# The last-but-one block is scaled as soon as its divisors are there, and VectorE's closing products all come before its closing sums

## The chip, the cores and the metric

The kernel runs on one core of a Trainium2 chip. The metric is the device time of one execution in microseconds, as a median over runs; the profile of one further execution shows where the time goes. Engines are named as in the profile: PE is TensorE (products), PEld its weight loads, DVE is VectorE, ACT is ScalarE, POOL is GpSimd, SP is SyncE, on whose queue nearly all transfers are issued.

## The reference

The input is one sequence of 2048 tokens with 640 features in bfloat16.

```python
xn = layernorm(x)
qkv = xn @ wqkv                              # 32 heads of width 20
o = softmax(q @ k^T * 20**-0.5) @ v
s = o @ wo
h = sigmoid(xn @ w_gate) * (xn @ w_up)       # 1728 wide
g = silu(h @ w_down)
out = x + s * g
```

## The kernel before, in words

**Tiling.** Attention is worked in 32 blocks. A block is one group of four heads (a group's heads stand on four bands of 32 partitions) and one chunk of 512 queries. Blocks 0 to 23 go group by group; the last eight blocks alternate between the last two groups, chunk by chunk, so that block 30 is group 6 and block 31 group 7, both of the last chunk. The loop over the blocks' score tiles (128 keys by 512 queries, L977) keeps three engines full: TensorE makes scores, ScalarE takes the exponent of most of them (L176, into `pu`), and VectorE takes the exponent of the rest by bit operations: one conversion to 16-bit integers (L1382, `iv`) and three passes over up to four tiles at a time (L1081, L1084, and the multiply L1087, into `pb`). TensorE then multiplies the exponents with the values (L1029); the row of sums comes out beside the results in the same PSUM bank.

**Scaling of a block.** When all products of a block are done, `norm_a` copies the bank to `on` and sends the row of sums through memory to a tile of 128 partitions (`ld`, `lt`). `norm_b` takes the reciprocals (L1053) and sends them back, spread over the bands, as `rl`, in four copies (L1058). `norm_c` multiplies `on` by `rl` into `on_bf` (L1066) and copies the result onwards. For blocks up to 29 GpSimd does the multiply; for block 30 VectorE does, and four copies (L1070) bring its 80 rows together in the tile `o6`. The profile calls both `o6` and the last block's `o7` by the name `o`.

**Order of the work.** It is neither the program's loops nor the hardware that decide in which order each engine meets its instructions: a planner in the kernel steps a model of TensorE, ScalarE and VectorE in steps of 0.01 us and writes out, at build time, what each engine is given next. The planner keeps a list `gos` of blocks that wait to be scaled, each with the time from which their `rl` is expected. On VectorE the scaling is one of several candidates, tried after the closing chain and after the copying of a finished bank, ahead of ready parts of other work (`active`: projections, the gated unit, out-projection) and of the exponent passes. It is taken if its time has come and, besides, two conversions are ready or will be within 0.3 us, or if 8 us (`GO_WAIT`; 1.5 us for some blocks) have gone by. The engines follow the written order strictly.

**Out-projection.** The first three chunks' output rows are done in parts of 128 by 320 (`mk_out`): five products (L847), then on VectorE a product with the gate (L854, `otmp`) and a sum with the input (L858, on VectorE for the last parts, on GpSimd for the earlier ones), then a copy out (L860). In the last chunk, groups 0 to 5 are multiplied early (`mk_part`, L884, L890, L892). What is left for the end of the run is:

- `e_on` (L1126): ScalarE copies the last block's bank.
- `e_tr` (L1130): four transposes on TensorE; `div_scale` (L818, L820): VectorE divides by the sums; `e_back` (L1139): four transposes back; `e_o` (L1143): ScalarE copies the result to `o7`, in the buffer of `rl`.
- `early` (L1117): eight products with block 30's `o6`: four of 128 columns into the bank `rest`, four of 512 into the banks `mains`. `late_mm` (L1121): the same eight with `o7`, added up in the same banks. `tail_banks` takes the banks that the out-projection used before.
- VectorE multiplies `rest` and `mains` with the gate (L1163 twice, L1170 four times, `hT`), and VectorE or GpSimd adds the input and the earlier groups' part (L1166 on GpSimd twice; L1173 for each of the four row tiles). Four copies (L1177), two issued by SP and two by ScalarE, write the last 512 rows.

The two places that the change touches:

```python
if eng == "DVE" and gos and gos[0][0] <= now and (
        sum(x[3] <= now + 0.3 for x in dq) >= 2 or now > gos[0][0] + (1.5 if pressing(gos[0][1]) else GO_WAIT)):
```

```python
add = nc.vector if t4 > 1 else nc.gpsimd
add.tensor_tensor(out=tail[t4][:, 0:512], in0=tmps[t4], in1=xps[t4][:, 0:512], op=ALU.add)
```

Of the kernel before, what the change touches and what calls it, by code (L numbers as in the profile page):

```python
# [145 lines left out]
def kernel(  # L146
# [11 lines left out]
    nc = tc.nc  # L158
# [346 lines left out]
    T_GO, GO_AT, GO_WAIT = 0.08, 9.0, 8.0  # L505
    gos, pool_at, pool_from = [], [0.0], [0.0]
# [7 lines left out]
    NBLK = NG * NQC  # L514
# [7 lines left out]
    def pressing(b):  # L522
        return b >= PAIR and b % 2 == 1
# [443 lines left out]
    def claim_dve(had, not_j):  # L967
        for b in range(base(), min(NBLK, base() + 2)):
            if q_at.get(b, 1e9) > now:
                return None  # L970
            if n_left[b] >= (rule["dl"] if b < NBLK - 1 else rule["dle"]):
                js = [j for j in range(GH) if left[b][j] and j not in not_j]
                return take(b, max(js, key=lambda j: (j not in had, len(left[b][j]), j)), -1) if js else None
        return None
# [86 lines left out]
    def norm_c(b, on, rl, sync):  # L1061
        g, c = gc(b)
        if sync:
            nc.vector.memset(rl[0:1, 0:1], 1.0)  # L1064
        on_bf = w2.tile([P, QC], BF16, tag="on_bf", bufs=2, name="on_bf")
        (nc.gpsimd if sync else nc.vector).tensor_tensor(out=on_bf, in0=on, in1=rl, op=ALU.mult)  # L1066
        if b == NBLK - 2:
            last["o6"] = wk.tile([P, QC], BF16, tag="aq", bufs=4, name="o6")[0:GC, :]
            for j in range(GH):
                nc.sync.dma_start(out=last["o6"][j * DH:(j + 1) * DH, :], in_=on_bf[32 * j + 1:32 * j + 1 + DH, :])  # L1070
            return
        for j in range(GH):
            f = g * GC + j * DH
            nc.sync.dma_start(out=oD[f:f + DH, c * QC:(c + 1) * QC], in_=on_bf[32 * j + 1:32 * j + 1 + DH, :])
# [36 lines left out]
    def tail_banks():  # L1111
        if not tb:
            tb.extend([f for f in range(NFX) if f != pv_bank[0]])
            mains[2], mains[3], rest[0] = [bank[f] for f in tb]
# [5 lines left out]
    def late_mm(dst, t4, sl):  # L1120
        nc.tensor.matmul(dst, lhsT=last["o"][:, t4 * P:(t4 + 1) * P], rhs=wo_t[1][0:GC, sl], start=False, stop=True,  # L1121
                         skip_group_check=True)
# [28 lines left out]
    def tail_steps():  # L1151
        tail_banks()
        for _, _, f in fill:
            f()
        for t4 in range(4):
            late_mm(rest[0][:, t4 * EX:(t4 + 1) * EX], t4, slice(512, D))
        for t4 in range(4):
            late_mm(mains[t4], t4, slice(0, 512))
        tmps = [hfl[:, t4 * 2 * D:t4 * 2 * D + 1024].bitcast(FP32) for t4 in range(4)]
        tmp = hfl[:, 8 * D:8 * D + 8 * EX].bitcast(FP32).rearrange("p (t e) -> p t e", e=EX)  # L1160
        rests = rest[0].rearrange("p (t e) -> p t e", e=EX)
        for i in range(2):
            nc.vector.scalar_tensor_tensor(out=tmp[:, 2 * i:2 * i + 2, :], in0=rests[:, 2 * i:2 * i + 2, :], scalar=0.25,  # L1163
                                           in1=gq_last[i].rearrange("p (t u) -> p t u", u=D)[:, :, 512:D],
                                           op0=ALU.mult, op1=ALU.mult)
            nc.gpsimd.tensor_tensor(out=xr_last[i][:, :, 512:D], in0=tmp[:, 2 * i:2 * i + 2, :],  # L1166
                                    in1=wdf.rearrange("p (t u) -> p t u", u=D)[:, 2 * i:2 * i + 2, 512:D], op=ALU.add)
        for t4 in range(4):
            gqr = gq_last[t4 // 2][:, t4 % 2 * D:t4 % 2 * D + 512]
            nc.vector.scalar_tensor_tensor(out=tmps[t4], in0=mains[t4], scalar=0.25, in1=gqr,  # L1170
                                           op0=ALU.mult, op1=ALU.mult)
            add = nc.vector if t4 > 1 else nc.gpsimd
            add.tensor_tensor(out=tail[t4][:, 0:512], in0=tmps[t4], in1=xps[t4][:, 0:512], op=ALU.add)  # L1173
        for i, t4 in enumerate((0, 2, 1, 3)):
            r = slice(4 * (NQC - 1) * P + t4 * P, 4 * (NQC - 1) * P + (t4 + 1) * P)
            eng = nc.sync if i % 2 == 0 else nc.scalar
            eng.dma_start(out=out2[r, :], in_=tail[t4])  # L1177

    with tc.manual_schedule(engines={ENG.PE, ENG.Activation, ENG.DVE}):
# [6 lines left out]
        now = 0.0  # L1186
# [3 lines left out]
        dq = []  # L1190
# [53 lines left out]
        while chain or timed or gos or items or glu_items or any(it.i < len(it.ops) for it in active):  # L1244
# [62 lines left out]
            for eng in ("ACT", "DVE"):  # L1307
# [13 lines left out]
                    norm_pending = None  # L1321
                    continue
                if eng == "DVE" and gos and gos[0][0] <= now and (
                        sum(x[3] <= now + 0.3 for x in dq) >= 2 or now > gos[0][0] + (1.5 if pressing(gos[0][1]) else GO_WAIT)):
                    _, b, on, rl = gos.pop(0)
                    norm_c(b, on, rl, b < NBLK - 2)
                    if b == NBLK - 2:
                        free["DVE"] = max(now, pool_at[0] if pool_from[0] <= now else now) + 0.60
                        ev_at[("o6",)] = free["DVE"] + 2.5
                        continue  # L1330
                    free["DVE"] = now + T_GO
                    pool_from[0] = max(pool_at[0], now + T_GO + 0.15)
                    pool_at[0] = pool_from[0] + 1.3
                    o_at[b] = pool_at[0] + 4.0
                    continue
# [8 lines left out]
                if eng == "ACT":  # L1344
                    s = slots[nexp % 2]
                    if nexp < nfill and s["a"] is not None and s["at"] <= now:
                        jobs = s["a"]
                        m = len(jobs)
                        if pu_run(m) is not None:
                            u = pu_take(m)  # L1350
                            end, x = now, u
# [71 lines left out]
            if free["PE"] <= now:  # L1423
# [57 lines left out]
                if nxt == "F":  # L1481
# [3 lines left out]
                    while len(d_new) < rule["dmax"] and (dcur is not None or buf_free(iv_left, NIV)) \  # L1485
# [4 lines left out]
                        x = claim_dve([t[2] for t in dcur["jobs"]] if dcur else [], [y[2][2] for y in d_new])  # L1490
# [78 lines left out]
        assert not items and not glu_items and not any(it.i < len(it.ops) for it in active)  # L1569
        assert not timed and not gos  # L1570
        tail_steps()

# [28 lines left out]
```

## Time and profile before

| | |
|---|---|
| device time, median of 3 runs | 797.38 us (796.93 to 799.03) |
| span of the profiled execution | 798.3 us |
| PE busy | 760.7 us, 95% |
| DVE busy | 771.0 us, 97% |
| ACT busy | 769.2 us, 96% |
| POOL busy | 83.0 us, 10% |
| mean granted TensorE clock | 0.99 |

Busy times are those of the whole span; they hardly tell the stages apart, since three engines are full in all but the last few microseconds. A stretch is read better from the timeline of each engine, from the list of waits (who waited, on what, how long) and from the chain that ended last: it starts at the last instruction and goes back to whatever released each step. In the profile, an instruction's start and its length are those of the engine's work; one instruction's end overlaps a little with the next one's start on VectorE, so the pace is read from start to start.

### The profile page before, as it was taken

How to read it: one execution, taken by the hardware profiler on the slowest of the kernel's cores; microseconds unless marked ns; L12 is line 12 of the kernel's file. 1: busy time of each engine (PE TensorE's matmuls, PEld its weight loads, DVE VectorE, ACT ScalarE, POOL GpSimd, SP SyncE). 2: the span in 40 equal slices, each digit the busy share in tenths (PEclk: the TensorE clock that was granted, in tenths of full speed). 3: DMA queues.
4: the chain of work that ended last, by engine and by line, in shares of the span. 5: the costliest groups of instructions: out<-in, count | busy, mean ns of one | idle time of the engine just before them, and what ended most of it. 6: DMA issues, size and time to landing. Idle time of an engine off the chain costs nothing.

```text
span 798.3 us, 17147 instructions
## 1 busy us (share of the span) xinstructions
PE 760.7 (95%) x6509; PEld 274.5 (34%) x6509; DVE 771.0 (97%) x1276; ACT 769.2 (96%) x830; POOL 83.0 (10%) x99
## 2 busy tenths in 40 slices
PE   7899999999999999999999999999999999999994
PEld 5523223333333223333332333333333223333332
DVE  8899999999999999999999999999999999999995
ACT  7799999999999999999999999999999999999990
POOL 6100000000100000000000010000000002213132
PEclk9999999999999999999999999999999999999996
DMA  6521212124122122331113223342122332414301
GB/s 168 153 70 48 69 53 54 52 61 107 54 74 67 52 69 76 85 85 56 45 56 85 82 57 90 95 132 85 40 78 70 83 92 75 141 52 139 101 23 63
DMA packets 95875, 62.61 MB, mean 78 GB/s; under 512 B 36388, under 2 KB 89684, under 8 KB 95792
## 3 DMA queue, kind: packets, MB, share of 16 engines
q1 hardware_dynamic: 95504, 61.18, 27.3%
q8 instruction: 51, 0.84, 0.4%
q14 instruction: 32, 0.26, 0.1%
q10 hardware_dynamic: 288, 0.33, 0.1%
HBM read 47.84 MB, written 13.55 MB: 77 GB/s over the span
## 4 chain that ended last, share of the span: by engine, by line
ACT 49%; PE 33%; DVE 9%; issue 5%; DMA 3%; SPq 1%; POOL 0%; ACTq 0%; DVEq 0%; POOLq 0%
ACT pu L176 44%; PE pst L977 11%; PE pst L750 7%; PE pst L1029 6%; PE pst L788 4%; ACT tnh L176 3%; DVE iv L1382 3%; DVE pb L1087 2%; PE pst L847 1%; PE pst L610 1%; ACT td L176 1%; DMA lt<-ld 1%; DVE pb L1081 1%; PE pst L718 1%; PE pst L884 1%
## 5 line engine op out<-in xcount | busy, mean ns | idle before, releaser
L176 ACT ACTIVATE pu<-pst 128x1024 bf16<-128x1024 f32 (+2 forms) x690 | 735.6, 1322 | 3.6 <-PE pst L977 3.4
L1382 DVE TENSOR_SCALAR iv<-pst 128x512 int16<-128x512 f32 x492 | 324.7, 681 | 6.3 <-PE pst L977 3.9
L977 PE MATMUL pst<-q,kT 32*128 32x512 bf16 x2048 | 272.1, 383 | 14.2 <-ACT pu L176 9.1
L1029 PE MATMUL pst<-pu,v 128*21 128x512 bf16 x1556 | 177.7, 382 | 0.3 <-ACT pu L176 0.2
L977 PEld LDWEIGHTS <-kT 32*128 32x128 bf16 x2048 | 82.0, 91 | 255.2 <-issue 244.0
L1029 PE MATMUL pst<-pb,v 128*21 128x512 bf16 x984 | 152.5, 382 | 0.2 <-DVE pb L1087 0.2
L1087 DVE TENSOR_TENSOR pb<-iv,pb 128x2048 bf16<-128x2048 bf16 x123 | 151.1, 1228 | 0.5
L750 PE MATMUL pst<-xnT,wgu 128*128 128x512 bf16 x520 | 143.7, 382 | 1.3 <-DVE iv L1382 0.4
L1066 POOL TENSOR_TENSOR on_bf<-on,rl 128x512 bf16<-128x512 f32 x30 | 38.4, 1281 | 635.3 <-DVE rl L1064 549.5
L1081 DVE TENSOR_SCALAR pb<-iv 128x2048 int16<-128x2048 int16 x123 | 84.6, 688 | 0.2 <-PE pst L1029 0.2
L788 PE MATMUL pst<-wd,hT 128*128 128x320 bf16 x448 | 84.1, 302 | 0.4 <-DVE iv L1382 0.3
L1084 DVE TENSOR_SCALAR pb<-iv 128x2048 int16<-128x2048 int16 x123 | 84.0, 683 | 0.0
L1029 PEld LDWEIGHTS <-v 128*21 128x21 bf16 x2540 | 49.4, 91 | 85.1 <-issue 62.7
L750 PEld LDWEIGHTS <-wgu 128*128 128x128 bf16 x520 | 38.5, 97 | 62.7 <-issue 40.5
L788 PEld LDWEIGHTS <-hT 128*128 128x128 bf16 x448 | 35.6, 97 | 40.7 <-issue 30.2
L610 PE MATMUL pst<-xnT,wu 128*128 128x512 bf16 x160 | 46.3, 383 | 0.1
L176 ACT ACTIVATE tnh<-pst 128x512 bf16<-128x512 f32 (+1 forms) x56 | 45.2, 808 | 0.0
L758 DVE SCALAR_TENSOR_TENSOR hT<-tnh,pst 128x512 bf16<-128x512 bf16 x52 | 35.3, 678 | 0.2
L718 PE MATMUL pst<-wv,xnT 128*128 128x160 bf16 x280 | 27.7, 239 | 1.4 <-DVE v L285 0.8
L718 PEld LDWEIGHTS <-xnT 128*128 128x128 bf16 x280 | 20.2, 100 | 11.2 <-issue 9.9
L847 PE MATMUL pst<-xnT,v 128*128 128x320 bf16 x120 | 21.0, 300 | 0.7 <-DVE otmp L890 0.5
L1043 DVE COPY on<-pst 128x512 f32<-128x512 f32 x31 | 21.1, 682 | 0.3 <-PE pst L1029 0.2
(115 smaller groups left out, 354.8 us busy)
## 6 DMA issues: line engine op xcount, KB each, us to landing
rl<-rd SPq DMA_DIRECT2D x124, 64.0 KB
wgu<-in_B_w_gate_dram SPq DMA_DIRECT2D x24, 320.0 KB
wgu<-in_B_w_up_dram SPq DMA_DIRECT2D x24, 320.0 KB
gq_dram<-gqs SPq DMA_DIRECT2D x24, 160.0 KB
xnT<-gq_dram SPq DMA_DIRECT2D x10, 320.0 KB
xt<-in_A_x_dram SPq DMA_DIRECT2D x16, 160.0 KB
oD<-on_bf SPq DMA_DIRECT2D x120, 20.0 KB
wd<-in_B_w_down_dram SPq DMA_DIRECT2D x1, 2080.0 KB
```

The lines of the kernel that those rows point to most:

```text
L176: return nc.scalar.add_instruction(mybir.InstActivation(func=func, name=nc.get_next_instruction_name(), engine=ENG.Activation, ins=[nc.sca ...
L610: nc.tensor.matmul(st["ps"], lhsT=wus[u][:, kd, i, :], rhs=xnT[:, c, kd, :], start=(kd == 0), stop=(kd == KD - 1))
L718: nc.tensor.matmul(st["ps"][:, i * 2 * GC:(i + 1) * 2 * GC], lhsT=xn_tok(tts[i], kd), rhs=wvs[pr][:, kd, :], start=(kd == 0), stop=(kd == ...
L750: nc.tensor.matmul(st[key][0:fs, :], lhsT=w[:, i, kd, ko * P:ko * P + fs], rhs=xnT[:, c, kd, :], start=(kd == 0), stop=(kd == KD - 1))
L788: nc.tensor.matmul(st["ps"][:, 0:HD], lhsT=hT[0:fsz[kf], kf, t4 * P:(t4 + 1) * P], rhs=wd[0:fsz[kf], kf, h * HD:(h + 1) * HD], start=(kf = ...
L977: nc.tensor.matmul(dst, lhsT=kTs[gc(b)[0] % 2][32 * j:32 * j + 32, kt * P:(kt + 1) * P], rhs=qts[b % 3][32 * j:32 * j + 32, :], start=True ...
L1029: nc.tensor.matmul(bank[pv_bank[0]][32 * j:32 * j + DH + 1, :], lhsT=lhsT, rhs=u["src"], start=first, stop=last, tile_position=(0, 32 * j) ...
L1066: (nc.gpsimd if sync else nc.vector).tensor_tensor(out=on_bf, in0=on, in1=rl, op=ALU.mult)
L1081: nc.vector.tensor_scalar(out=pb[:, 0, :, :].bitcast(I16), in0=iv, scalar1=0x7F80, scalar2=1, op0=ALU.bitwise_and, op1=ALU.bitwise_or)
L1084: nc.vector.tensor_scalar(out=pb[:, 1, :, :].bitcast(I16), in0=iv, scalar1=0x007F, scalar2=0x3F00, op0=ALU.bitwise_and, op1=ALU.bitwise_or)
L1087: nc.vector.tensor_tensor(out=pb[:, 1, :, :], in0=iv.bitcast(BF16), in1=pb[:, 1, :, :], op=ALU.mult)
L1382: nc.vector.tensor_scalar(out=d["iv"][:, j:j + w, :], in0=pst[:, F_POS[bk]:F_POS[bk] + w, :], scalar1=B_OFF, scalar2=0.0, op0=ALU.add, op1 ...
```

## The change

```diff
             gqr = gq_last[t4 // 2][:, t4 % 2 * D:t4 % 2 * D + 512]
             nc.vector.scalar_tensor_tensor(out=tmps[t4], in0=mains[t4], scalar=0.25, in1=gqr,
                                            op0=ALU.mult, op1=ALU.mult)
-            add = nc.vector if t4 > 1 else nc.gpsimd
+        for t4 in range(4):
+            add = nc.vector if t4 else nc.gpsimd
             add.tensor_tensor(out=tail[t4][:, 0:512], in0=tmps[t4], in1=xps[t4][:, 0:512], op=ALU.add)
-        for i, t4 in enumerate((0, 2, 1, 3)):
+        for i, t4 in enumerate((0, 1, 2, 3)):
...
                 if eng == "DVE" and gos and gos[0][0] <= now and (
-                        sum(x[3] <= now + 0.3 for x in dq) >= 2 or now > gos[0][0] + (1.5 if pressing(gos[0][1]) else GO_WAIT)):
+                        sum(x[3] <= now + 0.3 for x in dq) >= 2 or now > gos[0][0] + (1.5 if pressing(gos[0][1]) else GO_WAIT) or gos[0][1] == NBLK - 2):
```

It has two parts. In the planner, block 30 (`NBLK - 2`) is scaled as soon as its time in `gos` has come, whatever else VectorE has ready. In the last steps, VectorE makes its four large closing products (L1170) one after the other and only then adds; it takes three of the four large sums instead of two, so that GpSimd has one; and the output copies are issued in the order of the row tiles. The part at the end puts in one line, so lines behind it stand one further down in the changed kernel: L1173 becomes L1174, L1177 becomes L1178, L1382 becomes L1383.

## The prediction

> **What bounds the kernel now.** The page says that PE, DVE and ACT are each busy for 95 to 97% of the span, so no stage but an unbalanced one can be shortened by an edit this small. I therefore read three views of the end of the run, in this order: the chain of work that ended last, the waits, and the timelines of VectorE and of the DMA queue. The chain from 781.97 us on (start, length, what):
>
> ```profile
> 781.97 0.68 DVE on_bf L1066
> ...
> 785.09 1.91 DMA o<-on_bf
> ...
> 787.13 2.29 PE pst L1117 x8
> 789.42 0.44 PE pst L1121 x4
> 789.89 0.45 DVE hT L1163 x2
> ...
> 790.56 1.89 DVE hT L1170 x3
> 792.47 1.17 DVE xr L1173
> 793.64 0.61 DVE hT L1170
> 794.27 1.04 DVE xr L1173
> ```
>
> The end is one string: block 30 is scaled (L1066), its four copies to `o` are issued and land, the eight products L1117 and the eight L1121 follow, then VectorE's closing products and sums. It starts at the scaling. The waits of 770 to 799 us (who waited for whom: sum, times, longest) say what that costs:
>
> ```profile
> DVE hT L1163 <- PE pst L1121: 5.4, 1, 5.4
> PE pst L1117 <- DMA o<-on_bf: 4.7, 1, 4.7
> ACT o L1143 <- DVE on_bf L1066: 3.7, 1, 3.7
> ```
>
> VectorE stands still for 5.4 us and TensorE for 4.7 us, both because the scaling came late; ScalarE waits too, since its copy `o` reuses the buffer `rl` that the scaling reads. Was the scaling late because its data was late? The DMA queue and the stretches of half a microsecond (last two numbers: DMA share and GB/s; the third from the end is TensorE's clock) answer that:
>
> ```profile
> 769.84 1.71 SPq L1058 DMA_DIRECT2D rl<-rd  x4
> 782.68 3.12 SPq L1070 DMA_DIRECT2D o<-on_bf  x4
> ```
>
> ```profile
> 772.50:773.00 0.50, 0.50 (x10) 0.15 (x6) 0.50 (x1) 0.50 (x2) 0.00 (x0) 1.00 0.24 74
> 773.00:773.50 0.50, 0.50 (x6) 0.29 (x4) 0.47 (x2) 0.50 (x2) 0.00 (x0) 1.00 0.00 0
> ...
> 785.00:786.00 1.00, 0.00 (x0) 0.00 (x0) 0.00 (x0) 0.00 (x0) 0.00 (x0) 1.00 0.12 32
> 786.00:786.50 0.50, 0.00 (x0) 0.00 (x0) 0.00 (x0) 0.00 (x0) 0.00 (x0) 0.50 0.07 16
> ```
>
> The `rl` copies are issued from 769.84 us and nothing moves after 773.0, so the data was there nine microseconds before it was used. The second pair shows the clock halving near 786.0, after TensorE's last product ended at 782.41. And VectorE is full between (timeline):
>
> ```profile
> 773.04 1.23 DVE L1087 TENSOR_TENSOR pb<-iv,pb 128x2048 bf16<-128x2048 bf16 x1
> 774.18 0.48 DVE L854 SCALAR_TENSOR_TENSOR otmp<-pst,xnT 128x320 f32<-128x320 f32 x1
> 781.97 0.68 DVE L1066 TENSOR_TENSOR on_bf<-on,rl 128x512 bf16<-128x512 f32 x1
> 784.01 0.49 DVE L858 TENSOR_TENSOR wd<-otmp,wd 128x320 bf16<-128x320 f32 x1
> ```
>
> Its last work before the hole ends at 784.42 us (784.01 plus the usual 0.41 to the next start).
>
> **What the Trainium skill says.** "TensorE: Matmul & The Clock Gate", section "What's actually happening", says that about 3.4 us of idleness halve TensorE's clock; here it fell 3.6 us after the last product, which agrees. "SBUF — State Buffer", section "Who interferes with whom", says that a VectorE instruction with two SBUF inputs contends with a GpSimd instruction that reads SBUF, one with a single SBUF input does not. The trace agrees: L1066 (128x512, two SBUF inputs, GpSimd idle) takes 0.684 us, the same shape at L1173 takes 1.17 and 1.04 beside GpSimd's sums, while L1170, which reads PSUM and SBUF, stays at 0.679. "DMA: Bandwidth & Descriptors", section "Rules for kernel authors", advises to issue early and wait late; the 1.91 us of the last `o` copy, exposed now, are such a latency.
>
> **The change part by part.** I compared the two programs' instruction orders. Up to the VectorE multiply at 773.04 us they are alike on every engine, so only what follows can differ.
>
> *Scaling moved.* L1066 goes from behind the fifth of the last seven out-projection pairs (L854, L858) to ahead of the first. It starts at 774.18, where 773.04 ends; `rl` is there 1.2 us earlier, so the wait costs nothing. It takes 0.60 us there (781.97 to 782.57) and gives the same 0.60 back later. The copies' issues follow at 774.9 instead of 782.68; they took 3.12 us, the last starting 2.41 after the first, so the last starts at 777.3 and lands at 779.2. Behind them in the DMA queue stand only copies of finished output rows, for which no engine waits.
>
> *What the planner shifts with it.* The last multiply L1087 goes behind one more pair. VectorE from 774.18: scaling 0.60, pair 0.93 (774.18 to 775.11), L1081 and L1084 0.60 each, pair 0.97: L1087 runs from 777.88 to 779.1 instead of 776.43 to 777.66. The last four attention products wait for it and end near 779.6; before, they ended at 778.3. So `on` (0.59) is ready at 780.3 and the transposes L1130 (0.6) at 780.95, a full 1.2 us later. It costs nothing: VectorE has three pairs for that time, 779.02 to 781.86, and all products they need are issued. The 128x1536 exp becomes two (by the means of the rows 0.81 + 1.21 for 1.67, so 0 to 0.35 us); ScalarE ended at 777.8 and has until 779.1, so I take nothing.
>
> *New order at the end.* From 781.86: reciprocal and scaling of the last block (L818, L820) 0.69, to 782.55; two pairs, 1.86, to 784.4: VectorE's work is the same sum as before. L1139 transposes 782.65 to 783.1, `o` of the last block is copied 783.2 to 783.8. L1117 finds its data long there; its order of waits shows that its second 512-wide product needs the PSUM bank that the last L854 reads, which starts near 783.5 and releases at 784.0. From 784.05 three 512-wide products at 0.22 and four 128-wide at 0.07 give 785.0 (full-clock paces: five 128x512 products of L750 take 1.19 us in the chain and four 0.97; the four of L1139 take 0.42, one 0.23; at half clock the timeline has 0.42 and about 0.11), and with 0.2 us of latency L1163 starts at 785.2. Before: 789.89. That is 4.7 us earlier; 0.8 us of VectorE's hole stay. TensorE's longest rest is now about half a microsecond, so I take the full clock; half clock would add 3 × 0.2 + 4 × 0.04, about 0.8, and is the upper bound.
>
> *Closing products ahead of closing sums.* Before, 5.42 us pass from 789.89 to the end of the last sum at 795.31. After: two L1163 0.67, four L1170 at 0.62, 2.5, then three sums instead of two. GpSimd has one sum instead of two: it starts its small ones 0.57 after L1163, needs 1.36 for them and 1.3 for the large one, so ends 3.2 us after L1163 started, just when VectorE's first sum starts. The sums then take what L1066 takes: 0.60 + 0.60 + 0.68 = 1.9. Together 5.1, a gain of 0.3; if they still collide as now (1.1 each), 6.4, a loss of 1.0. I take 5.1, since GpSimd is done. The four output copies follow at 0.6 us; the last had 3.0 us from its sum's end to the end of the span, and I keep that.
>
> Sum: 4.7 + 0.3 = 5.0 us. 797.38 − 5.0 = 792.4.
>
> **The rivals.** (A) *TensorE still at half clock, or sums that still collide with GpSimd*: 0.8 or 1.0 us back, 793.2 to 793.4, both 794.2. For it: there are only some 20 short products between 782.4 and 785. Against: clock 1.00 for the 3.6 us of full idleness before. (B) *The output copies become the bound*: four of 160 KB issued in 1.9 us instead of 2.2; they moved at up to 300 GB/s, 0.55 us each, but 164 to 191 while draining, 0.86 each. A backlog of 0.3 to 1.0 gives 792.7 to 793.4. (C) *VectorE has no hole left*: L1163 at 784.5, 791.7. (D) *A new wait takes the old one's place*: the scaling, now early in a strict order, waits for `rl`; the multiplies for attention and all pairs stand behind it, TensorE waits for those, and the end moves one for one. To give no change (797.4) `rl` must land 1.2 + 5.0 = 6.2 us later than in the trace, to end slower by 0.3% (799.8) 8.6 us later. Against it stands the DMA silence from 773.0.
>
> **How the numbers follow.** Forecast 0.60 (791.9 to 793.0), A 0.14, B 0.10, C 0.10, D 0.06. The range 791.1 to 794.4 takes in C less 0.6 and both halves of A with 0.2 to spare (the runs of before lie 2.1 us apart, their median less uncertain); it leaves out D, A and B together, and some of C's low side, less than 2 in 10. The 0.3% lines are 795.0 and 799.8: faster takes all but D, 0.94; D is split into 0.04 the same and 0.02 slower.
>
> **What would show it.** Right: no wait of TensorE for `o<-on_bf`; L1066 near 774.2 with no idle before it; the `o` copies issued by 778; clock 1.00 at L1121; L1163 at 785.2 with VectorE idle about 0.8 before it; three VectorE sums at 0.7; span about 793.3. Wrong: idle VectorE before L1066, a last L1087 later than 779, a half clock at L1117, sums still near 1.1 us, or over 3.0 us from the last sum to the end.

## The result, and the profile after

| | before | after |
|---|---|---|
| device time, median of 4 runs | 797.42 us (796.93 to 799.03) | 792.61 us (791.69 to 793.10) |
| ratio, with its 95% interval | | 0.9935 (0.9918 to 0.9952) |
| span of the profiled execution | 798.3 us | 791.4 us |
| from the start of the instruction behind the last common L1087 (774.18 before, 772.59 after) to the end of the span | 24.1 us | 18.8 us |

The kernel is 4.8 us faster. The two spans differ by 6.9 us, but 1.6 us of that lie ahead of the first instruction that the change moves: the common L1087 started at 773.04 before and at 771.45 after, and at 773.13 in a second profile of the changed kernel. That is mostly scatter from one execution to the next: the profiled execution of the kernel before took 800.0 us, 2.6 above its median, and that of the changed kernel 793.1, 0.5 above. All comparisons below count from the scaling (L1066) or from the first closing product (L1163).

The chain that ended last, from the scaling on (start, length, what):

```profile
772.06 0.53 issue
772.59 0.69 DVE on_bf L1066
...
781.38 0.49 DVE wd L858
781.87 0.41 DVE otmp L854
782.28 0.04 issue
782.32 0.81 PE pst L1117 x3
783.13 0.24 PE pst L1121 x4
...
784.14 2.39 DVE hT L1170 x4
786.53 0.61 DVE xr L1174
```

The copies to `o` and the eight products L1117 after them are gone from it. Between the scaling and 782.28 stands VectorE's own work, and only three products L1117 are left: the one that waits for the last L854, and the two behind it. The waits from 770 us on (who, on whom: sum, times, longest):

```profile
ACT o L1143 <- PE pst L1139: 2.9, 1, 2.9
DVE hT L1163 <- PE pst L1121: 0.6, 1, 0.6
PE pst L1117 <- DVE otmp L854: 0.3, 1, 0.3
```

VectorE's 5.4 us ahead of L1163 are 0.6; TensorE's 4.7 us for `o<-on_bf` have left the list; ScalarE waits for TensorE's transposes, no longer for the scaling. The DMA queue, a stretch (third number from the end: TensorE's clock) and the timelines of VectorE and, in the last line, GpSimd:

```profile
768.54 1.71 SPq L1058 DMA_DIRECT2D rl<-rd  x4
773.30 3.10 SPq L1070 DMA_DIRECT2D o<-on_bf  x4
```

```profile
783.00:784.00 1.00, 1.00 (x9) 0.48 (x7) 0.61 (x2) 0.00 (x0) 0.04 (x1) 1.00 0.33 120
```

```profile
772.59 0.69 DVE L1066 TENSOR_TENSOR on_bf<-on,rl 128x512 bf16<-128x512 f32 x1
776.25 1.22 DVE L1087 TENSOR_TENSOR pb<-iv,pb 128x2048 bf16<-128x2048 bf16 x1
783.39 0.75 DVE L1163 SCALAR_TENSOR_TENSOR hT<-pst,gql 128x256 f32<-128x256 f32 x2 [0.60 <-PE pst L1121]
784.06 2.47 DVE L1170 SCALAR_TENSOR_TENSOR hT<-pst,gql 128x512 f32<-128x512 f32 x4
786.46 1.89 DVE L1174 TENSOR_TENSOR xr<-hT,wd 128x512 bf16<-128x512 f32 x3
```

```profile
785.32 1.27 POOL L1174 TENSOR_TENSOR xr<-hT,wd 128x512 bf16<-128x512 f32 x1
```

The `o` copies are issued by 776.4, and the first L1117 starts at 781.40; TensorE is at full clock when it makes L1121; three sums take 1.89 us together, where two took 1.17 and 1.04 before. GpSimd's one large sum ends at 786.59 us, 0.13 after VectorE's first begins.

### The profile page after: what moved, and what is told of

Same layout as the page of the kernel before. It is cut to its first block, busy times and chain, and to the rows that moved or that the text cites. A ratio compares the mean times of both kernels' runs of the same rounds, so it can differ in the third digit from the quotient of the medians.

```text
span 791.4 us, 17148 instructions
## 1 busy us (share of the span) xinstructions
PE 756.8 (96%) x6509; PEld 272.6 (34%) x6509; DVE 770.5 (97%) x1277; ACT 768.5 (97%) x831; POOL 81.4 (10%) x98
## 4 chain that ended last, share of the span: by engine, by line
ACT 50%; PE 33%; DVE 9%; issue 5%; DMA 1%; SPq 1%; POOL 0%; DVEq 0%; ACTq 0%; POOLq 0%
ACT pu L176 45%; PE pst L977 11%; PE pst L750 7%; PE pst L1029 5%; PE pst L788 4%; ACT tnh L176 3%; DVE iv L1383 2%; DVE pb L1087 2%; PE pst L610 2%; PE pst L847 1%; ACT td L176 1%; DVE pb L1081 1%; DVE pb L1084 1%; PE pst L884 1%; DVE xn L384 0%
## 5 line engine op out<-in xcount | busy, mean ns | idle before, releaser
L1383 DVE TENSOR_SCALAR iv<-pst 128x512 int16<-128x512 f32 x492 | 324.8, 681 | 5.2 <-PE pst L977 2.9
L1087 DVE TENSOR_TENSOR pb<-iv,pb 128x2048 bf16<-128x2048 bf16 x123 | 151.3, 1230 | 0.5
L1066 POOL TENSOR_TENSOR on_bf<-on,rl 128x512 bf16<-128x512 f32 x30 | 38.4, 1280 | 633.4 <-DVE rl L1064 564.0
L1084 DVE TENSOR_SCALAR pb<-iv 128x2048 int16<-128x2048 int16 x123 | 83.9, 682 | 0.0
L847 PE MATMUL pst<-xnT,v 128*128 128x320 bf16 x120 | 21.1, 301 | 0.7 <-DVE otmp L890 0.5
```

The lines of the kernel that those rows point to most:

```text
L1084: nc.vector.tensor_scalar(out=pb[:, 1, :, :].bitcast(I16), in0=iv, scalar1=0x007F, scalar2=0x3F00, op0=ALU.bitwise_and, op1=ALU.bitwise_or)
L1087: nc.vector.tensor_tensor(out=pb[:, 1, :, :], in0=iv.bitcast(BF16), in1=pb[:, 1, :, :], op=ALU.mult)
L1383: nc.vector.tensor_scalar(out=d["iv"][:, j:j + w, :], in0=pst[:, F_POS[bk]:F_POS[bk] + w, :], scalar1=B_OFF, scalar2=0.0, op0=ALU.add, op1 ...
```

## The experiments

The kernels ran in three jobs, each on one chip and timed beside the kernel before, whose median was 798.76, 798.29 and 797.82 us in them. Where two variants are compared by time, they are of the same job unless the text says otherwise. A diff is against the changed kernel unless it says otherwise.

### The changed kernel once more

> The changed kernel itself, as the measure for the other three runs. Both theories: 792.4 us and within 1 us of it; from the start of the scaling of block 30 to the start of the first closing product (L1163) 10.8 us, from there to the end of the last closing sum 5.0 us.

792.99 us (791.27 to 795.91) against 798.76 before, ratio 0.9927 (0.9902 to 0.9952). Scaling at 774.27, L1163 at 785.06, end of the last sum at 790.02: 10.8 and 5.0 us. This is the measure for the other kernels of the first job: the scaling alone, the closing order alone, and, further below, the kernel that takes away the wait that is left.

### The scaling alone

```diff
-        for t4 in range(4):
-            add = nc.vector if t4 else nc.gpsimd
+            add = nc.vector if t4 > 1 else nc.gpsimd
...
-        for i, t4 in enumerate((0, 1, 2, 3)):
+        for i, t4 in enumerate((0, 2, 1, 3)):
```

> The planner's part alone; the closing products and sums stay in the order of before, two sums on GpSimd. Theory (the late scaling held up the end): 792.5 to 793.1 us, that is 4.4 to 4.9 below the kernel before; 10.8 us from the scaling to L1163, then 5.4 us to the end of the last sum, VectorE's two large sums at 1.0 to 1.2 us each. Rival (the closing order brings most of the gain, the scaling only moves a wait): 796 to 797 us, with a wait of some 4 us on TensorE or VectorE at another place.

793.61 us (792.77 to 796.53), ratio 0.9935 (0.9912 to 0.9957): 5.2 us below the kernel before, where the whole change brings 5.8 in the same job. Both this gain and the time lie somewhat above what was expected. Its timeline at the end:

```profile
782.64 0.76 DVE L1163 SCALAR_TENSOR_TENSOR hT<-pst,gql 128x256 f32<-128x256 f32 x2 [0.60 <-PE pst L1121]
785.22 1.16 DVE L1173 TENSOR_TENSOR xr<-hT,wd 128x512 bf16<-128x512 f32 x1
787.02 1.04 DVE L1173 TENSOR_TENSOR xr<-hT,wd 128x512 bf16<-128x512 f32 x1
```

The scaling is at 771.85, so L1163 follows after 10.8 us, and the last sum ends 5.4 us after that. The scaling alone brings nearly all, so the rival is wrong.

### The closing order alone

```diff
-... or gos[0][1] == NBLK - 2):
+...):
```

> The order of the closing products and sums alone; block 30 is scaled where it was before. Theory: 796.9 to 797.2 us, 0.2 to 0.5 below the kernel before, not to be told from it; TensorE still waits 4.7 us for the copies to o and VectorE 5.4 us; L1163 to the end of the last sum 5.0 us instead of 5.4, sums at 0.6 to 0.7 us. Rival (the closing order brings most of the gain): 793 to 794 us.

798.24 us (797.28 to 800.34), ratio 0.9994 (0.9980 to 1.0007): no difference that can be measured, though the median is 0.5 us lower. Its two large waits are those of the kernel before, number for number:

```profile
DVE hT L1163 <- PE pst L1121: 5.4, 1, 5.4
PE pst L1117 <- DMA o<-on_bf: 4.7, 1, 4.7
```

L1163 starts at 789.74 and the last sum ends at 794.69: 5.0 us, as forecast. In this one profile the span ends 3.5 us after that, where all other profiles of the study have 2.96 to 3.05. Its cause is open; the closer output copies don't explain it, since the changed kernel issues them as closely and has 3.05.

### Who makes the closing sums

Three kernels change only the last lines of the changed one: two sums on GpSimd, none, and each sum right behind its product. The first diff shows two of them, one added line each.

```diff
-            add = nc.vector if t4 else nc.gpsimd
+            add = nc.vector if t4 > 1 else nc.gpsimd    # two_gpsimd_sums
+            add = nc.vector                             # no_gpsimd_sum
```

```diff
-        for t4 in range(4):
             add = nc.vector if t4 else nc.gpsimd        # sums_between: in the loop of the products
```

> The changed kernel with two of the four large closing sums on GpSimd, as before, but all products still ahead of the sums. Theory (the two engines hold each other up when both sum from SBUF): VectorE's two sums take 1.0 to 1.2 us each, GpSimd's second ends near the end, L1163 to the end of the last sum 5.2 to 5.4 us, 0.2 to 0.4 longer than in the changed kernel; 792.7 us. Rival (the order alone makes the difference, no contention): VectorE's sums at 0.6 to 0.7 us, GpSimd ends last, 4.6 us after L1163 starts; 792.0 us.

> The changed kernel with all four large closing sums on VectorE; GpSimd keeps its two small ones. Theory: four sums at 0.6 us each with no contention, L1163 to the end of the last sum 5.6 us, 0.6 longer than in the changed kernel; 793.0 us. Rival (GpSimd's one large sum still slows VectorE's products or sums): 5.0 to 5.2 us.

> The changed kernel with each large sum right behind its product, still one sum on GpSimd and three on VectorE. Theory (a sum that comes early meets GpSimd's, and one right behind its product waits for it): VectorE's first sum takes 1.0 to 1.3 us, the others 0.6 to 0.7, with gaps of 0.1 between product and sum; L1163 to the end of the last sum 5.4 to 5.9 us, 0.4 to 0.9 longer than in the changed kernel; 793 us. Rival (only the number of sums on GpSimd matters): 5.0 to 5.2 us, 792.5 us.

| | L1163 to end of last sum | time, ratio to before |
|---|---|---|
| changed kernel | 5.0 us | 792.99, 0.9927 (0.9902 to 0.9952), first job |
| two sums on GpSimd | 5.4 us | 792.56, 0.9939 (0.9916 to 0.9963) |
| no large sum on GpSimd | 5.5 us | 792.92, 0.9945 (0.9926 to 0.9964) |
| sums between the products | 6.4 us | 793.72, 0.9950 (0.9935 to 0.9965) |

The times lie too close to be told apart, so the traces decide. First two sums on GpSimd (VectorE's two sums in one line, then GpSimd's two; the third line has the shortest, median and longest of VectorE's two, in ns):

```profile
785.79 2.35 DVE L1174 TENSOR_TENSOR xr<-hT,wd 128x512 bf16<-128x512 f32 x2
```

```profile
784.66 2.93 POOL L1174 TENSOR_TENSOR xr<-hT,wd 128x512 bf16<-128x512 f32 x2
```

```profile
L1174 DVE TENSOR_TENSOR xr<-hT,wd x2: 682/1213/1744, 785.8 to 786.4; 128x512 bf16<-128x512 f32 x2
```

With the products first but two sums on each engine, VectorE's two take 2.35 us together, while three in the changed kernel take 1.89. They don't take 1.0 to 1.2 each, as expected: the first takes 0.68, and the second 1.74, since it meets GpSimd's second. The kernel with the scaling alone differs from this one only in the order of the products and of the output copies, and has the same 5.4 us; the end of the span follows 3.04 and 2.96 us later. So neither order brings anything by itself. The sum taken from GpSimd does, and only with the products first, so that GpSimd is all but done when VectorE begins to sum: with each sum right behind its product, one sum on GpSimd makes the stretch 6.4 us, longer than two do. Giving GpSimd none costs 0.6 us, one sum's length. The case between the products shows the collision itself (VectorE's first sum, its next, and GpSimd's):

```profile
784.56 1.76 DVE L1173 TENSOR_TENSOR xr<-hT,wd 128x512 bf16<-128x512 f32 x1
...
786.96 0.69 DVE L1173 TENSOR_TENSOR xr<-hT,wd 128x512 bf16<-128x512 f32 x1
```

```profile
784.51 1.26 POOL L1173 TENSOR_TENSOR xr<-hT,wd 128x512 bf16<-128x512 f32 x1
```

GpSimd started 0.05 us earlier and finished in 1.26 us, as undisturbed in the changed kernel (1.27); VectorE's sum took 1.76 and ended 0.55 us after GpSimd's, where a whole one takes 0.69. I had expected 1.0 to 1.3 and a stretch of at most 5.9 us: a sum that starts just behind GpSimd's waits for nearly all of it.

### A scaling that comes before its data

```diff
-gos.append((now + (7.0 if pressing(tm[1]) or tm[1] == NBLK - 2 else GO_AT), ...
+gos.append((now + (7.0 if pressing(tm[1]) else 3.0 if tm[1] == NBLK - 2 else GO_AT), ...
```

> The changed kernel with block 30's time in the planner's list 4 us earlier, so that its scaling stands four conversions and three passes ahead of its place, before its divisors rl have landed. Theory (VectorE's order is strict, and a scaling that waits holds up all behind it): VectorE is idle for 2.5 to 3.0 us before L1066, the products for attention and all that follows come so much later, and the time is 794.5 to 795.5 us. Rival (there is slack behind the scaling that takes in such a wait): idle before L1066, but 792.5 to 793.0 us.

796.99 us (795.32 to 798.88), ratio 0.9982 (0.9973 to 0.9991): of the change's gain, 5.8 and 5.3 us in the two other jobs, 1.3 us are left. 794.5 to 795.5 us had been expected. The scaling in the timeline, then the waits:

```profile
771.66 0.69 DVE L1066 TENSOR_TENSOR on_bf<-on,rl 128x512 bf16<-128x512 f32 x1 [2.95 <-DMA rl<-rd]
```

```profile
ACT pu L176 <- PE pst L977: 3.9, 3, 2.8
PE pst L977 <- DVE iv L1383: 3.2, 1, 3.2
DVE on_bf L1066 <- DMA rl<-rd: 2.9, 1, 2.9
DVE hT L1163 <- PE pst L1121: 1.0, 1, 1.0
```

The wait of 2.95 us came as expected, but cost more than it lasted. From the start of the L1087 that is the last instruction common to both (767.50 here, 767.80 in the changed kernel) to L1163 it is 19.70 us instead of 15.59: 4.1 us lost. Behind the scaling on VectorE stand two conversions L1383 (not four, as the expectation has it); TensorE waits 3.2 us for the banks that they empty, and ScalarE 3.9 us for TensorE's scores. The planner also gave all eight L1117 a place behind the last L854 (VectorE waits 1.0 us instead of 0.6 for their successors). Of the 1.1 us beyond the wait itself, VectorE's timeline shows these 0.4 and a new wait of 0.35 us for a product L847; the last 0.4 lie in small gaps whose cause is open. I had counted only VectorE's own wait.

The same trace measures what the change lives on: when `rl` is really there. Its chain reads:

```profile
767.80 0.32 SPq L1058
...
769.10 2.43 DMA rl<-rd
...
771.66 0.69 DVE on_bf L1066
```

From the first `rl` issue to the scaling that waits for it, 3.86 us pass. In the ten other profiles in which the scaling has its new place it starts 4.05 to 4.60 us after that issue. So it stands 0.2 to 0.7 us behind its data, if the landing takes as long as in this one trace.

### The wait that is left

```diff
-    fill += [... for t4 in (2, 3, 0, 1)]
+    fill += [... for t4 in (2, 0, 1, 3)]
...
+        hold = fill.pop()[2]
         for _, _, f in fill:
             f()
...
-        for t4 in range(4):
+        for t4 in range(3):
             late_mm(mains[t4], t4, slice(0, 512))
+        hold()
+        late_mm(mains[3], 3, slice(0, 512))
```

> The changed kernel, but the one product of L1117 that waits for the bank which the last L854 reads is issued at the very end, together with its partner of L1121; the 128-wide products of L1121 go ahead of it. Theory (the 0.6 us that VectorE still waits are the wait for this bank, passed on by TensorE's order): the wait before L1163 falls from 0.6 to 0.1 us or less, L1163 starts 10.2 us after the scaling, the time is 791.8 to 792.0 us, 0.5 to 0.6 below the changed kernel. Rival (VectorE waits for the copy of the last block to o, or for the latency of the products): the wait stays at 0.4 us or more and the time is that of the changed kernel.

> The kernel late_bank_last once more, beside the next. Theory: 0.6 to 0.7 us below the changed kernel in the median, no wait before L1166 in the profile, 10.1 us from the scaling to it. Rival: no difference.

> The changed kernel, as the measure for the two runs above: 792.4 to 793.0 us, 0.6 us of idle VectorE before L1163, 10.8 us from the scaling to it.

The first closing product (L1166 here; the kernel has three more lines) now follows the last L858 with no wait:

```profile
782.21 0.49 DVE L858 TENSOR_TENSOR wd<-otmp,wd 128x320 bf16<-128x320 f32 x1
782.62 0.75 DVE L1166 SCALAR_TENSOR_TENSOR hT<-pst,gql 128x256 f32<-128x256 f32 x2
```

The scaling starts at 772.50, so 10.1 us instead of 10.8; the second profile repeats it (772.61 to 782.73), and the third of the changed kernel has 10.8 again, with 0.59 us of wait. The wait was the bank, then, passed on by TensorE's order to products that don't need it. The medians show it less well: 792.27 us (790.76 to 796.01) against 792.99 in the first job, 792.41 (791.04 to 793.01) against 792.53 (791.94 to 792.94) in the third, 0.1 us where 0.6 to 0.7 had been expected. The sign is as expected in both jobs, but the runs overlap, and a gain in time is not shown.

### Taking work off VectorE

```diff
-            st["v"] = n_left[NBLK - 1] <= (NJOB // 2 if h == 1 else NJOB // 4)
+            st["v"] = False                             # on top of late_bank_last
```

> The kernel late_bank_last with, besides, all sums of the out-projection (L858) on GpSimd, which was idle there, so that VectorE has seven sums of 0.41 us and the gaps before them less. Theory (from the scaling on, VectorE's own work sets the end): from the start of the scaling to the end of the last closing sum 14.0 to 14.6 us, against 15.1 in late_bank_last and 15.8 in the changed kernel; VectorE's passes L1081, L1084 and L1087 take 0.1 to 0.4 us more where they meet GpSimd; time 790.8 to 791.6 us. Rival (contention with GpSimd and the attention's end take the place of VectorE's own work): 15 us or more, the time of late_bank_last or worse.

790.88 us (790.75 to 791.55), ratio 0.9913 (0.9899 to 0.9926); the changed kernel in the same job took 792.53, and the two sets of runs don't overlap. Its own base, late_bank_last, took 792.41. From the scaling (772.23) to the end of the last sum (786.74) it is 14.5 us, against 15.1 in the base and 15.8 in the changed kernel. One pass pays for it, and new waits appear:

```profile
773.84 1.28 DVE L1084 TENSOR_SCALAR pb<-iv 128x2048 int16<-128x2048 int16 x1
...
777.86 0.49 DVE L854 SCALAR_TENSOR_TENSOR otmp<-pst,wd 128x320 f32<-128x320 f32 x1 [0.81 <-PE pst L847]
...
781.79 0.76 DVE L1166 SCALAR_TENSOR_TENSOR hT<-pst,gql 128x256 f32<-128x256 f32 x2 [0.54 <-PE pst L1121]
```

L1084 takes 1.28 instead of 0.69 us beside a GpSimd sum that started at 773.40; and with seven sums fewer VectorE waits for TensorE in four places, 2.2 us in all. This is the fastest version of the study. It shows that in its base VectorE's own work set the end, but only up to some 0.6 us: of the seven sums, 0.41 us each, most comes back as waits for TensorE and as the longer pass. For the changed kernel itself, the chain above shows the same: VectorE's work from the scaling to the last L854.

## Why the prediction was right

792.4 us was forecast, 792.6 measured. An agreement to 0.2 us is partly luck: the gain, forecast as 5.0, was 4.8, 5.8 and 5.3 us in the three sets of runs that have both kernels, and 5.3 in the two traces, counted from the scaling's new place. Step by step:

- *The scaling was late for no reason of its data, and all behind it was late with it.* Shown by the scaling alone (5.2 us) and by the unchanged 5.4 and 4.7 us of waiting without it. By the 3.86 us that the copies of `rl` took in the kernel that scales too early, the data was there 8.3 us before its use, not nine.
- *4.7 us up to L1163.* From the scaling's new place to L1163: 11.0 us forecast, 10.8 measured three times; it was 15.7 from that point before. So the gain was 4.9; the wait that stayed was 0.6 us, not 0.8, and its reason, the bank of the last L854, is shown by the kernel that takes it away.
- *Attention ends 1.2 us later, at no cost.* Counted from the scaling's place, L1087 was to end after 4.9 us and ended after 4.9 (777.47). ScalarE's copy `on` was to be done after 6.1 and was done after 6.0 (778.59). VectorE has no wait between.
- *Full clock for the closing products.* It was 1.00 through 783 to 784 us. Rival A had 0.8 us for half clock and 1.0 for the collision; neither came. Its second price was too low: 6.4 us in place of the 5.1 forecast is 1.3, so the collision would have meant 793.7 us, and both together 794.5, just outside the range given.
- *5.1 us for products and sums.* 4.96 measured. The reason was as assumed: GpSimd has one sum, and VectorE's sums come after it. Both parts are needed: the order without the sum taken from GpSimd leaves 5.4 us, that sum without the order makes it 6.4. The times resolve none of these differences; the traces alone show them.
- *3.0 us from the last sum to the end.* 3.05; rival B's backlog did not show. (The closing order alone had 3.5 in its one profile, cause open.)
- *The wait for `rl` costs nothing, with 1.2 us to spare.* The first half held; the 1.2 us did not. I read the landing off the moment when the transfers fell silent. Where the scaling waits, it starts about half a microsecond after that (the stretch from 771.0 to 771.5 moved 8 GB/s, the scaling started at 771.66). Counted from the first issue of the copies, the margin is 0.2 to 0.7 us, if the landing takes as long as in that one trace. Rival D (6 per cent) was thus nearer than its working made it, and its price was too low as well: it counted the delay one for one, and a wait of 2.95 us cost 4.1.

## What to carry to other kernels

A planner that fills an engine's gaps can treat a short instruction as one more filler while a whole chain (here four copies, eight products and the closing work) hangs on it; at the end of a run, where no later block hides the chain, such an instruction should go as soon as its data is there. "As soon as" has an edge: in a strict order a wait is paid by everything queued behind it and by the engines that this feeds (here 4.1 us for a wait of 2.95), so measure when the semaphore comes rather than when the last byte moves, and leave a margin. When two engines share the last sums, count what each still has to do when the other begins: an even split took 0.4 us more here than three to one, by the traces.

## What the runs showed of the hardware that was not expected

A VectorE sum that started 0.05 us after a GpSimd sum of the same shape took 1.76 us instead of 0.69, while GpSimd's took its undisturbed 1.26: the later one waited for nearly all of the earlier one. This is what the Trainium skill, "SBUF — State Buffer", section "Who interferes with whom", describes as an exclusive lock for the whole instruction. Before the change, with sums that met only in part, 1.04 and 1.17 us had looked like a mutual slowing. They fit the lock as well. GpSimd's two sums in the kernel before (together, then shortest, median and longest in ns):

```profile
791.82 2.94 POOL L1173 TENSOR_TENSOR xr<-hT,wd 128x512 bf16<-128x512 f32 x2
```

```profile
L1173 POOL TENSOR_TENSOR xr<-hT,wd x2: 1268/1492/1717, 791.8 to 793.0; 128x512 bf16<-128x512 f32 x2
```

They end at 793.09 and 794.76 us, and VectorE's two end at 793.64 and 795.31: each 0.55 us behind the GpSimd sum that it met, as in the case of 1.76 us. GpSimd's second, 1.72 us instead of 1.27, met VectorE's first, which had begun before it.

The one-input pass L1084 was held up in the same way (1.28 instead of 0.69 us, again ending 0.55 us behind the GpSimd sum). The same section excepts instructions with at most one SBUF input only outside VectorE's two-port modes; whether L1084 runs in such a mode is not shown by these traces.
